# Experts 1 to 7: the first layer as seven block products in place of eight, in three passes over the tokens

## The chip, the cores and the metric

The kernel runs on one core of a Trainium2 chip, alone. The metric is the device time of one execution in microseconds (us), the median of three runs. Its engines are TensorE (PE, whose weight loads the profile shows apart as PEld), VectorE (DVE), ScalarE (ACT), GpSimd (POOL) and SyncE (SP, which issues all DMAs here). Each takes its instructions strictly in the order in which the program gives them; they wait for each other by semaphores.

## What is computed

Sparse attention feeds a mixture of experts with a Sinkhorn gate. Cut to what matters (x has 2304 rows, D = 512, 8 experts, F = 1024, all float32):

```python
x = attention(q, k, v)                  # 4 batches x 576 positions, 8 heads x 64
P = sinkhorn(exp(x @ w_gate), 8 rounds) # over all 2304 tokens
for e in range(8):
    h = np.maximum(x @ w1[e], 0.0)      # first layer, 512 -> 1024
    out += P[:, e:e + 1] * (h @ w2[e])  # second layer, 1024 -> 512
```

## The kernel before

Every operand of a large product is held as two float32r numbers, a high part (a copy that rounds) and a low part (the rest), and a product is three matmuls: high by high, high by low, low by high. The first layer of one f tile (128 columns of F) for a chunk of tokens is 4 blocks of D by 3 = 12 matmuls into one PSUM bank (`layer1`, L324 to L341); ACT writes relu's high part, DVE its low part. The second layer (`layer2`, L343 to L372) takes 3 matmuls for each 128 tokens and adds up four f tiles in a bank.

A unit is four f tiles, half an expert: 16 units. Unit 0 takes tokens in 9 chunks of 256; units 1 to 15 in four chunks of 512 and one of 256, which stands third (last in unit 15). A slot is one f tile of one chunk: `layer1` of this slot, then `layer2` of the slot before (L434 to L457). The attention of all batches (32 steps) is woven into the prologue and the first 26 slots of unit 0, the gate's 28 pieces into the 28 slots after those. Weights are loaded piece by piece through four raw buffers and split once each by ACT (L125) and POOL (L126) in the last chunk of the unit before. `xhi` and `xlo` hold all tokens in SBUF for the whole run (L95, L96); `acc` holds the output (L97).

The order on each engine is the order in which the code calls it (`manual_schedule`, L84); nothing moves it.

Of the kernel before, what the change touches and what calls it, by code (L numbers as in the profile page):

```python
# [14 lines left out]
S = 576  # L15
# [36 lines left out]
def kernel(  # L52
# [16 lines left out]
    FH = 4  # f tiles of a unit (half an expert)  # L69
# [30 lines left out]
    pieces = [(u, ft, which) for u in range(NU) for ft in range(FH) for which in range(2)]  # L100
# [3 lines left out]

    def load_w():
        nonlocal n_loaded
        if n_loaded == len(pieces):
            return
        u, ft, which = pieces[n_loaded]
        n_loaded += 1  # L110
        e, fh = divmod(u, UPE)
        f0 = (fh * FH + ft) * P
        t = raw_p.tile([P, D], F32, tag="raw", name=f"raw{which}_{u}_{ft}")
        if which == 0:
            t = t.rearrange("p (k f) -> p k f", f=P)
            nc.sync.dma_start(t, w1[e, :, f0 : f0 + P].rearrange("(k p) f -> p k f", p=P))
        else:
            nc.sync.dma_start(t, w2[e, f0 : f0 + P, :])
        raw[u, ft, which] = t

    def split_w(u, ft, which):
        src = raw.pop((u, ft, which))
        shape = [P, 2, NDT, P] if which == 0 else [P, 2, D]
        t = wt_p.tile(shape, F32R, tag=f"w{which + 1}", name=f"w{which + 1}_{u}_{ft}")
        nc.scalar.activation(t[:, 0], src, AF.Copy)  # L125
        nc.gpsimd.tensor_tensor(t[:, 1], src, t[:, 0].bitcast(F32), op=ALU.subtract)  # L126
        wt[u, ft, which] = t
        load_w()

# [1 line left out]
    # A tile holds, for a local pair, 64 queries of each head (partition halves) by the 96 keys of  # L131
    # their window; for a strided pair, one head's queries by keys of a group of residues.
# [5 lines left out]
    def load_qkv(k):  # L138
        if k < NS:
            nq, nk, nv = _columns(*steps[k][1:])  # L140
            t = qkv_p.tile([P, QK], F32, tag="qk", name=f"qk_{k}", bufs=3)
            nc.sync.dma_start(t[:, : nq + nk], qkv[k, :, : nq + nk])
            tv = qkv_p.tile([P, 5 * 2 * DH], F32, tag="v", name=f"v_{k}", bufs=5)
            nc.sync.dma_start(tv[:, :nv], qkv[k, :, nq + nk : nq + nk + nv])
            qkv_t[k] = t, tv[:, :nv].rearrange("p (w j d) -> p w j d", j=2, d=DH)

    def at_scores(k):
# [17 lines left out]
        else:  # L165
# [3 lines left out]
            # The heads use different row halves of the array and different banks. The first  # L169
            # batch takes one head after the other, so that its softmax starts sooner.  # L170
# [12 lines left out]
        for j, (sc, masks, n, rows, nk) in enumerate(res):  # L183
            sm = at_p.tile([P, 5 * KW], F32, tag="sm", name=f"sm_{k}_{j}", bufs=6)
# [14 lines left out]
            sms[k].append((sm, sums[:rows, j * n : (j + 1) * n], n, rows, nk))  # L199
# [11 lines left out]
    def at_transpose(k):  # L211
        pts[k] = []
        for j, (sm, _, n, rows, nk) in enumerate(sms.pop(k)):
            pt = at_p.tile([P, 5, P], F32, tag="pt", name=f"pt_{k}_{j}")
# [8 lines left out]
    def at_values(k, tag):  # L223
# [3 lines left out]
        if _is_local(p):  # L227
# [9 lines left out]
            src = pv[:, : n * QT]  # L237
            dst = [x[:, p, c0 : c0 + n * QT] for x in (xhi, xlo)]
        else:
            r0, nr, n = SGROUPS[hf]  # L240
            m = nr * NJ
            for i in range(n):
                for j in range(2):
# [6 lines left out]
            dst = [  # L250
                x[:, p, b * S : (b + 1) * S].rearrange("p (j r) -> p j r", r=STRIDE)[
                    :, :, r0 : r0 + nr * n
                ]
                for x in (xhi, xlo)
            ]
        nc.scalar.activation(dst[0], src, AF.Copy)  # L256
        nc.vector.tensor_tensor(dst[1], src, dst[0].bitcast(F32), op=ALU.subtract)  # L257

# [1 line left out]
    def gate_logits(c0, n):  # L260
        pl = ps.tile([P, 4 * P], F32, tag="t", name=f"pl_{c0}")
        for dt in range(NDT):
            for i, x in enumerate((xhi, xlo)):
                nc.tensor.matmul(  # L264
                    pl[:, :n], wgs[:, 2 * E * dt : 2 * E * dt + P], x[:, dt, c0 : c0 + n],
                    start=(dt == 0 and i == 0), stop=(dt == NDT - 1 and i == 1),
                )
        nc.vector.tensor_copy(lt[:, :n], pl[: 2 * E, :n])
# [55 lines left out]
    def layer1(u, c, ft):  # L324
# [11 lines left out]
        h = h_p.tile([P, 2, 4 * P], F32R, tag="h", name=f"h_{u}_{c0}_{ft}")  # L336
# [6 lines left out]
    def layer2(u, c, ft):  # L343
# [8 lines left out]
        for i in range(nt):  # L352
# [6 lines left out]
            if ft == FH - 1:  # L359
                t = c0 // P + i  # L360
                e = u // UPE
                if u == 0:
                    nc.scalar.activation(acc[:, t, :], y, AF.Copy)
                elif e == 0:
                    nc.vector.tensor_tensor(acc[:, t, :], y, acc[:, t, :], op=ALU.add)
                else:
                    nc.vector.scalar_tensor_tensor(  # L367
                        acc[:, t, :], y, gate[:, t, e : e + 1], acc[:, t, :],
                        op0=ALU.mult, op1=ALU.add,
                    )  # L370
                if u == NU - 1:
                    nc.sync.dma_start(out[t * P : (t + 1) * P, :], acc[:, t, :])  # L372

# [18 lines left out]
    def attention_values(tag="t"):  # L392
        if 0 <= at_k - LAG < NS:
# [13 lines left out]
    for k in range(2 * NP - 2 + LAG):  # L407
# [3 lines left out]
        if 1 <= k <= 2 * FH:  # L411
            split_w(*pieces[k - 1])
# [7 lines left out]

    slots = []
    for u in range(NU):
        if u == 0:
            chunks = [(c, 256) for c in range(0, NT, 256)]
        else:
            chunks = [(c, min(512, NT - c)) for c in range(0, NT, 512)]
            if u < NU - 1:
                chunks.insert(2, chunks.pop())
# [3 lines left out]
    bg = None  # L432
    prev = None
    for u, c, ft, last in slots + [(None, None, None, False)]:  # L434
        if u is not None:
            layer1(u, c, ft)
            if last and u + 1 < NU:
                split_w(u + 1, ft, 0)
# [4 lines left out]
        if u == UPE and ft == 2:  # L443
            for t in range(c[0] // P, (c[0] + c[1]) // P):
                nc.vector.tensor_scalar_mul(acc[:, t, :], acc[:, t, :], gate[:, t, 0:1])
        if prev is not None:
            pu, pc, pft, plast = prev
            layer2(pu, pc, pft)
            if plast and pu + 1 < NU:
# [7 lines left out]
        prev = (u, c, ft, last) if u is not None else None  # L457
# [79 lines left out]
```

## Time and profile before

| what | value |
|---|---|
| median of 3 runs | 1687.38 us (1685.89 to 1687.57) |
| the profiled execution, first to last instruction | 1686.0 us |
| TensorE busy | 1670.7 us, 99% |
| DVE, ACT, POOL busy | 494.6, 336.3, 200.2 us |
| mean granted TensorE clock | 0.996 of full speed |

A matmul row in a timeline has a start and a length; matmuls overlap, so the pace is read from one start to the next. The chain of waits is followed back from the last instruction: who ended last at each step. A window is a stretch of the span with each engine's busy time in it.

### The profile page before, as it was taken

The numbers are of one execution on the slowest core, as the hardware profiler recorded it, in microseconds if no ns is written. First come the engines' busy times: TensorE is split into PE (matmuls) and PEld (weight loads), VectorE is DVE, ScalarE is ACT, GpSimd is POOL, SyncE is SP. The second block draws the span as 40 slices with busy tenths as digits, with TensorE's granted clock in tenths as the row PEclk, the third lists the DMA queues.
The fourth block names the chain that finished last, engine by engine and source line by source line (L and its number), as shares of the span: only waits on it lengthen the run. The fifth ranks groups of instructions, "written<-read, shape, count | busy, mean of one in ns | idle before, by whom it ended". The sixth has DMA issues, their size and how long they took to land.

```text
span 1686.0 us, 20710 instructions
## 1 busy us (share of the span) xinstructions
PE 1670.7 (99%) x8611; PEld 1402.1 (83%) x8611; DVE 494.6 (29%) x1162; ACT 336.3 (20%) x824; POOL 200.2 (12%) x182
## 2 busy tenths in 40 slices
PE   7999999999999999999999999999999999999999
PEld 5888888888888888888888888888888888888887
DVE  4654244233222222222222222222222222222222
ACT  5554211112121111212111121211112121111211
POOL 4221200102020010202001020200102020010200
PEclk8999999999999999999999999999999999999999
DMA  6431100101010010101001010100101010010011
GB/s 208 127 104 50 45 7 13 38 1 51 0 45 7 13 39 0 51 0 44 7 14 38 1 50 1 44 7 13 37 1 51 1 44 7 13 38 1 26 50 63
DMA packets 55582, 56.80 MB, mean 34 GB/s; under 512 B 3904, under 2 KB 39744, under 8 KB 55488
## 3 DMA queue, kind: packets, MB, share of 16 engines
q1 hardware_dynamic: 55488, 55.47, 11.0%
q8 instruction: 68, 1.11, 0.3%
q14 instruction: 26, 0.21, 0.0%
HBM read 50.74 MB, written 4.72 MB: 33 GB/s over the span
## 4 chain that ended last, share of the span: by engine, by line
PE 98%; DMA 0%; POOL 0%; ACT 0%; DVE 0%; issue 0%; SPq 0%; POOLq 0%; ACTq 0%; DVEq 0%
PE ph L331 47%; PE y L355 47%; PE tp L219 1%; PE sc L159 1%; PE pv L232 1%; PE sc L176 1%; PE pl L264 0%; PE pv L244 0%; ACT sm L195 0%; DMA cst<-in_consts 0%; DMA qk<-in_qkv 0%; POOL w L126 0%; POOL sm L207 0%; PE pg L273 0%; DVE sm L189 0%
## 5 line engine op out<-in xcount | busy, mean ns | idle before, releaser
L355 PE MATMUL y<-w,h 128*128 128x512 f32 x3456 | 843.2, 391 | 0.0
L331 PE MATMUL ph<-xhi,w 128*128 128x512 f32 (+1 forms) x2688 | 787.8, 360 | 0.0
L355 PEld LDWEIGHTS y<-w,h 128*128 128x128 f32 x3456 | 642.5, 188 | 131.9
L331 PEld LDWEIGHTS ph<-xhi,w 128*128 128x128 f32 x2688 | 487.3, 189 | 77.4
L338 DVE SCALAR_TENSOR_TENSOR h<-ph,h 128x512 fp32r<-128x512 f32 (+1 forms) x336 | 206.8, 616 | 1110.1 <-ACT h L337 1110.1
L331 PE MATMUL ph<-xlo,w 128*128 128x512 f32 (+1 forms) x1344 | 482.6, 359 | 0.0
L337 ACT ACTIVATE h<-ph 128x512 fp32r<-128x512 f32 (+1 forms) x336 | 180.3, 537 | 1198.0 <-PE ph L331 1190.7
L126 POOL TENSOR_TENSOR w<-raw,w 128x512 fp32r<-128x512 f32 x128 | 164.7, 1287 | 1275.5 <-ACT w L125 1275.5
L331 PEld LDWEIGHTS ph<-xlo,w 128*128 128x128 f32 x1344 | 254.1, 189 | 39.6
L367 DVE SCALAR_TENSOR_TENSOR acc<-y,gate,acc 128x512 f32<-128x512 f32 x252 | 172.1, 743 | 1.2 <-PE y L355 1.2
L125 ACT ACTIVATE w<-raw 128x512 fp32r<-128x512 f32 x128 | 80.3, 627 | 101.2 <-POOL w L126 69.4
L195 ACT ACTIVATE sm<-sm,mx 128x96 f32<-128x96 f32 (+2 forms) x152 | 56.3, 372 | 33.5 <-DVE mx L189 33.5
L207 POOL TENSOR_TENSOR sm<-sm,sums 126x252 f32<-126x252 f32 (+3 forms) x48 | 35.2, 747 | 112.4 <-DVE sums L205 89.0
L189 DVE CUSTOM_DVE_ANT_0 sm<-sc,cst 128x96 f32<-128x96 f32 (+2 forms) x152 | 31.4, 264 | 12.2 <-DMA cst<-in_consts 5.9
L220 DVE COPY pt<-tp 126x252 f32<-126x252 f32 (+3 forms) x56 | 25.8, 494 | 20.0 <-PE tp L219 19.8
L195 ACT ACTIVATION_READ_ACCUMULATOR sm<-sm,mx 128x1 f32 (+2 forms) x152 | 28.4, 187 | 0.0
L219 PE MATMUL tp<-cst,sm 128*96 128x128 f32 (+2 forms) x152 | 23.8, 288 | 1.9 <-POOL sm L207 1.5
L219 PEld LDWEIGHTS tp<-cst,sm 128*96 128x96 f32 (+2 forms) x152 | 17.9, 139 | 7.7 <-POOL sm L207 3.5
L176 PE MATMUL sc<-qk 64*108 64x108 f32 (+1 forms) x160 | 15.9, 316 | 6.5 <-DMA qk<-in_qkv 4.2
L176 PEld LDWEIGHTS sc<-qk 64*108 64x108 f32 (+1 forms) x160 | 12.7, 208 | 8.6 <-DMA qk<-in_qkv 3.5
L257 DVE TENSOR_TENSOR xlo<-pv,xhi 128x252 fp32r<-128x252 f32 (+3 forms) x32 | 14.7, 458 | 15.0 <-ACT xhi L256 13.5
L159 PE MATMUL sc<-qk 64*64 64x96 f32 x288 | 17.6, 271 | 1.2 <-DMA qk<-in_qkv 1.2
(46 smaller groups left out, 185.2 us busy)
## 6 DMA issues: line engine op xcount, KB each, us to landing
raw<-in_w SPq DMA_DIRECT2D x128, 256.0 KB, 2.7
out<-acc SPq DMA_DIRECT2D x18, 256.0 KB, 2.0
qk<-in_qkv SPq DMA_DIRECT2D x8, 336.0 KB, 3.4
qk<-in_qkv SPq DMA_DIRECT2D x8, 324.0 KB, 3.1
v<-in_qkv SPq DMA_DIRECT2D x8, 320.0 KB, 2.9
qk<-in_qkv SPq DMA_DIRECT2D x8, 256.0 KB, 2.9
v<-in_qkv SPq DMA_DIRECT2D x8, 256.0 KB, 2.7
qk<-in_qkv SPq DMA_DIRECT2D x8, 252.0 KB, 3.1
```

The source lines that it names most:

```text
L125: nc.scalar.activation(t[:, 0], src, AF.Copy)
L126: nc.gpsimd.tensor_tensor(t[:, 1], src, t[:, 0].bitcast(F32), op=ALU.subtract)
L159: nc.tensor.matmul(sc[QT * j : QT * j + QT, i, :], t[sl, q0 : q0 + QT], t[sl, k0 : k0 + KW], start=True, stop=True,)
L176: nc.tensor.matmul(scs[j][:m, i, :m], t[sl, i * m : (i + 1) * m], t[sl, nq + i * m : nq + (i + 1) * m], start=True, stop=True,)
L195: nc.scalar.activation(sm[:, i, :], sm[:, i, :], AF.Exp, bias=mx[:rows, i : i + 1], scale=-1.0, accum_out=sums[:rows, j * n + i : j * n + ...
L207: nc.gpsimd.tensor_tensor(sm, sm, rs.unsqueeze(2).to_broadcast([rows, n, nk]), op=ALU.mult)
L219: nc.tensor.transpose(tp[:nk, i, :rows], sm[:, i0 + i, :], ident[:rows, :rows])
L331: nc.tensor.matmul(ph[:, :n], w[:, i, dt, :], x[:, dt, c0 : c0 + n], start=(k == 0), stop=(k == 3 * NDT - 1),)
L337: nc.scalar.activation(h[:, 0, :n], ph[:, :n], AF.Relu)
L338: nc.vector.scalar_tensor_tensor(h[:, 1, :n], ph[:, :n], 0.0, h[:, 0, :n].bitcast(F32), op0=ALU.max, op1=ALU.subtract)
L355: nc.tensor.matmul(y, h[:, a, i * P : (i + 1) * P], w[:, b, :], start=(ft == 0 and first), stop=(ft == FH - 1 and a == 1),)
L367: nc.vector.scalar_tensor_tensor(acc[:, t, :], y, gate[:, t, e : e + 1], acc[:, t, :], op0=ALU.mult, op1=ALU.add,)
```

## The change

Units 0 and 1 (expert 0) stay as they are. For experts 1 to 7 the first layer is cut in 2 by 2 blocks: x into token halves by halves of D, w1 into halves of D by halves of F. With s1 = x21 + x22, s2 = s1 - x11, s3 = x21 - x11, s4 = x12 - s2 and t1 = w12 - w11, t2 = w22 - t1, t3 = w12 - w22, t4 = w21 - t2, seven products and sums of their results give the four blocks of h that eight took.

- Tokens go in three passes of 768 (halves of 384, `TN`), and in each pass experts 1 to 7 go through in groups of two f tiles (one of each half of F): 3 x 7 x 4 = 84 groups. A group (`first`) has 7 products of 6 matmuls with 384 columns, and between them, as `fill(0)` to `fill(5)`, the second layer of the group before (`second`): 6 token tiles of 6 matmuls with 512 columns.
- DVE joins the products (`plus`, five times a group) and writes four low parts of relu; ACT copies one product and writes four high parts; DVE adds each of the 6 second-layer results to `acc` right away.
- w1 and w2 are loaded and split anew in each pass. POOL makes the t's of a group (three subtractions) and the low halves of w1's seven operands (four subtractions) and of two w2 tiles (two).
- x is written to DRAM (`store_x`, 2 MB for 512 tokens) as attention ends a chunk. While the gate runs, `build_s` makes the s's in six steps, one for each pass and each half of the 128-row blocks: four loads of x from DRAM, one POOL addition of 1536 columns (high plus low), four of 384, then an ACT copy of 1536 columns and a POOL subtraction of 1536, and two stores. One of its three parts runs at the end of each slot, from the 27th slot of unit 0 on. The region `reg` that held x then takes two sets of w1 operands and seven x operands, loaded for each pass by `load_x`.

```diff
+    def build_s(p, k):
+        st = pools["sb"].tile([P, 4, 2, TN], F32, tag="sx", name=f"sx_{p}_{k}", bufs=1)
+        t0 = 2 * TN * p
+        for i, (dh, th) in enumerate(((0, 0), (0, 1), (1, 1), (1, 0))):
+            nc.sync.dma_start(
+                st[:, i], xd[:, :, k + 2 * dh, t0 + TN * th : t0 + TN * (th + 1)]
+            )
+        yield
+        x, s = st[:, :, 0, :], st[:, :, 1, :]
+        nc.gpsimd.tensor_tensor(x, x, s, op=ALU.add)
...
+            nc.gpsimd.tensor_tensor(s[:, i, :], a, b, op=op)
+        yield
+        so = pools["sb"].tile([P, 2, 4, TN], F32R, tag="so", name=f"so_{p}_{k}", bufs=1)
+        split(so[:, 0], so[:, 1], s)
+        for i in range(2):
+            nc.sync.dma_start(sd[:, p, :, i, k, :], so[:, i].bitcast(F32))
+        yield
...
+    def prep_w1(g):
...
+        nc.gpsimd.tensor_tensor(
+            t, b[:, 0:1, :].to_broadcast([P, 2, 2 * P]), a, op=ALU.subtract
+        )
+        nc.gpsimd.tensor_tensor(u[:, 0], a[:, 1], t[:, 0], op=ALU.subtract)
+        nc.gpsimd.tensor_tensor(u[:, 1], b[:, 1], u[:, 0], op=ALU.subtract)
+        split(w[:, 0, 0:2], w[:, 1, 0:2], ra)
+        yield
+        split(w[:, 0, 4:6], w[:, 1, 4:6], ru)
+        yield
+        split(w[:, 0, 2:4], w[:, 1, 2:4], rt)
+        yield
+        split(w[:, 0, 6], w[:, 1, 6], rb[:, 1])
+        yield
...
+    def first(g, fill):
...
+        load_w1g(g + 2)
+        load_w2g(g + 1)
+        mul("w11", "x11", ba, True)
+        nc.scalar.activation(m1, A, AF.Copy)
+        mul("t2", "s2", bb, True)
+        plus(u2, B, m1)
+        mul("t1", "s1", bc, True)
+        fill(0)
+        w1n, w2n = prep_w1(g + 1), prep_w2(g)
+        mul("w21", "x12", ba, False)
+        relu_hi(0, 0, A)
+        relu_lo(0, 0, A)
+        next(w1n, None)
+        fill(1)
+        mul("t3", "s3", bb, False)
+        plus(u3, B, m1)
+        plus(u3, C, u3)
+        relu_hi(1, 1, u3)
+        next(w1n, None)
+        fill(2)
+        relu_lo(1, 1, u3)
+        fill(3)
+        mul("t4", "x22", bb, False)
+        plus(m1, B, m1)
+        relu_hi(1, 0, m1)
+        mul("w22", "s4", bc, False)
+        plus(u2, C, u2)
+        relu_hi(0, 1, u2)
+        relu_lo(1, 0, m1)
+        relu_lo(0, 1, u2)
+        next(w1n, None)
+        next(w2n, None)
+        fill(4)
+        next(w1n, None)
+        next(w2n, None)
+        fill(5)
...
             if at_k == NS + LAG:
-                bg = gating()
-        elif bg is not None:
-            next(bg, None)
+                store_x()
+                stacks["right"].close()
+                pools["sb"] = ctx.enter_context(tc.tile_pool(name="sb", bufs=1, side="right"))
+                bg = [gating(), sums()]
+        else:
+            for x in bg:
+                next(x, None)
+            if u == 1 and c[0] == 0 and ft == 0:
+                bg.append(early())
```

The change moves instructions at three places that matter below.

ACT, last chunks of unit 0, before (`h` is relu's high part of tokens from 1792 on, f tile by f tile; `acc` the copy of unit 0's result):

```order
L337 ACTIVATE h_0_1792_0_2395<-ph_0_1792_0_2382 128x256
L363 ACTIVATE acc_93<-y_0_1536_0_2314 128x512
L363 ACTIVATE acc_93<-y_0_1536_1_2315 128x512
L337 ACTIVATE h_0_1792_1_2429<-ph_0_1792_1_2416 128x256
L337 ACTIVATE h_0_1792_2_2459<-ph_0_1792_2_2446 128x256
L337 ACTIVATE h_0_1792_3_2491<-ph_0_1792_3_2478 128x256
L337 ACTIVATE h_0_2048_0_2519<-ph_0_2048_0_2506 128x256
```

and after (`so` is the split sum, first number the pass, second the half):

```order
L386 ACTIVATE h_0_1792_0_2469<-ph_0_1792_0_2456 128x256
L411 ACTIVATE acc_96<-y_0_1536_0_2371 128x512
L411 ACTIVATE acc_96<-y_0_1536_1_2372 128x512
L155 ACTIVATE so_0_0_2490<-sx_0_0_2418 128x1536
L386 ACTIVATE h_0_1792_1_2508<-ph_0_1792_1_2495 128x256
L386 ACTIVATE h_0_1792_2_2543<-ph_0_1792_2_2530 128x256
L386 ACTIVATE h_0_1792_3_2580<-ph_0_1792_3_2567 128x256
L155 ACTIVATE so_0_1_2595<-sx_0_1_2525 128x1536
L386 ACTIVATE h_0_2048_0_2613<-ph_0_2048_0_2600 128x256
```

The copies of the sums now stand between the relu's, one for three slots.

POOL at the same place, where before it had nothing between the last attention step (`sm`) and the splits of unit 1's weights; after:

```order
L245 TENSOR_TENSOR sm_31_0_2217<-sm_31_0_2217,sums_31_2216 128x480
L463 TENSOR_TENSOR sx_0_0_2418<-sx_0_0_2418 128x4x384
L471 TENSOR_TENSOR sx_0_0_2418<-sx_0_0_2418 128x384 x4
L156 TENSOR_TENSOR so_0_0_2490<-sx_0_0_2418,so_0_0_2490 128x1536
L463 TENSOR_TENSOR sx_0_1_2525<-sx_0_1_2525 128x4x384
L471 TENSOR_TENSOR sx_0_1_2525<-sx_0_1_2525 128x384 x4
L156 TENSOR_TENSOR so_0_1_2595<-sx_0_1_2525,so_0_1_2595 128x1536
L156 TENSOR_TENSOR w1_1_0_2616<-raw0_1_0_387,w1_1_0_2616 128x512
L156 TENSOR_TENSOR w1_1_1_2660<-raw0_1_1_495,w1_1_1_2660 128x512
L156 TENSOR_TENSOR w2_1_0_2673<-raw1_1_0_441,w2_1_0_2673 128x512
L463 TENSOR_TENSOR sx_1_0_2639<-sx_1_0_2639 128x4x384
```

The chain of additions and subtractions of a step stands ahead of the weight splits that follow it.

PE in the expert loop, after, one group (`ba`, `bb`, `bc` are the banks of the products, `yg` the second layer of the group before; before, 12 matmuls of `layer1` alternate with 12 of `layer2`):

```order
L555 MATMUL ba_20_6380<-reg_97 128x384 x6
L555 MATMUL bb_20_6381<-reg_97 128x384 x6
L555 MATMUL bc_20_6382<-reg_97 128x384 x6
L572 MATMUL yg_19_0_6413<-w2g_19_0_6349,h00_19_6230 128x512 x3
L572 MATMUL yg_19_0_6413<-w2g_19_1_6362,h01_19_6231 128x512 x3
L555 MATMUL ba_20_6380<-reg_97 128x384 x6
L572 MATMUL yg_19_1_6436<-w2g_19_0_6349,h00_19_6230 128x512 x3
L572 MATMUL yg_19_1_6436<-w2g_19_1_6362,h01_19_6231 128x512 x3
L555 MATMUL bb_20_6381<-reg_97 128x384 x6
```

The second layer of a group follows three products after the end of that group's own products.

## Rows read from the trace of the kernel before

**Rows 1.** The page's first part (busy us, share of the span, instructions) and the engine line of its chain that ended last.

```profile
PE 1670.7 (99%) x8611; PEld 1402.1 (83%) x8611; DVE 494.6 (29%) x1162; ACT 336.3 (20%) x824; POOL 200.2 (12%) x182
...
PE 98%; DMA 0%; POOL 0%; ACT 0%; DVE 0%; issue 0%; SPq 0%; POOLq 0%; ACTq 0%; DVEq 0%
```

**Rows 2.** Chain of waits in order of time: the 12 second-layer matmuls behind the chunk of 256 in units 2 and 3 (start, length, what).

```profile
347.85 2.75 PE y L355 x12
446.17 2.75 PE y L355 x12
```

**Rows 3.** Timeline of PE and its weight loads in unit 2 (start us, length, engine, line, form, count): 12 matmuls of 512 columns of layer 1, 12 of layer 2, 12 of 256 columns of layer 1, 12 of layer 2; each PE row is the first of its kind, and one weight load stands between.

```profile
340.81 0.39 PE L331 MATMUL ph<-xhi,w 128*128 128x512 f32 x1
...
343.53 2.88 PE L355 MATMUL y<-w,h 128*128 128x512 f32 x12
...
346.25 0.28 PE L331 MATMUL ph<-xhi,w 128*128 128x256 f32 x1
346.26 0.19 PEld L331 LDWEIGHTS ph<-xlo,w 128*128 128x128 f32 x1
...
347.69 2.91 PE L355 MATMUL y<-w,h 128*128 128x512 f32 x12
```

**Rows 4.** Groups of instructions with shapes kept apart (line, engine, operation, tile, shapes, count, busy us, mean ns of one, idle before).

```profile
L367 DVE SCALAR_TENSOR_TENSOR acc<-y,gate,acc 128x512 f32<-128x512 f32 x252 | 172.1, 743 | 1.2 <-PE y L355 1.2
...
L126 POOL TENSOR_TENSOR w<-raw,w 128x512 fp32r<-128x512 f32 x128 | 164.7, 1287 | 1275.5 <-ACT w L125 1275.5
...
L337 ACT ACTIVATE h<-ph 128x512 fp32r<-128x512 f32 x240 | 143.5, 598 | 956.2 <-PE ph L331 952.7 <-DVE g L298 3.5
...
L125 ACT ACTIVATE w<-raw 128x512 fp32r<-128x512 f32 x128 | 80.3, 627 | 101.2 <-POOL w L126 69.4 <-PE y L355 31.8
...
L337 ACT ACTIVATE h<-ph 128x256 fp32r<-128x256 f32 x96 | 36.8, 383 | 241.8 <-PE ph L331 238.0 <-DVE g L295 3.8
...
L207 POOL TENSOR_TENSOR sm<-sm,sums 126x252 f32<-126x252 f32 x16 | 9.4, 606 | 34.0 <-DVE sums L205 17.2 <-ACT sm L195 8.7 <-ACT acc L363 8.1
...
L207 POOL TENSOR_TENSOR sm<-sm,sums 128x480 f32<-128x480 f32 x8 | 7.9, 988 | 27.3 <-DVE sums L205 25.7 <-DVE wgs L416 1.6
```

**Rows 5.** The same view for DVE alone: two shapes of a subtraction with one input in PSUM.

```profile
L257 DVE TENSOR_TENSOR xlo<-pv,xhi 128x320 fp32r<-128x320 f32 x8 | 3.9, 490 | 2.8 <-ACT xhi L256 2.8
...
L257 DVE TENSOR_TENSOR xlo<-pv,xhi 128x256 fp32r<-128x256 f32 x8 | 3.4, 425 | 3.9 <-ACT xhi L256 3.0
```

**Rows 6.** Timeline around 300 to 306 us in unit 2's first slots: relu's high part on ACT, the split of a weight on ACT and POOL, and from 305.23 the last of 12 matmuls and the relu that waits for it.

```profile
300.21 0.60 ACT L337 ACTIVATE h<-ph 128x512 fp32r<-128x512 f32 x1 [2.04 <-PE ph L331]
300.71 0.62 ACT L125 ACTIVATE w<-raw 128x512 fp32r<-128x512 f32 x1
...
301.41 1.28 POOL L126 TENSOR_TENSOR w<-raw,w 128x512 fp32r<-128x512 f32 x1 [1.86 <-ACT w L125]
...
305.23 0.39 PE L331 MATMUL ph<-xhi,w 128*128 128x512 f32 x1
...
305.65 0.60 ACT L337 ACTIVATE h<-ph 128x512 fp32r<-128x512 f32 x1 [2.04 <-PE ph L331]
```

**Rows 7.** Timeline of DVE's scaling of `acc` (L445, four instructions in each row) without POOL at work and with it, and of POOL at the second place.

```profile
372.57 1.67 DVE L445 TENSOR_SCALAR acc<-acc,gate 128x512 f32<-128x512 f32 x4
...
394.29 1.29 POOL L126 TENSOR_TENSOR w<-raw,w 128x512 fp32r<-128x512 f32 x1 [1.86 <-ACT w L125]
394.33 3.81 DVE L445 TENSOR_SCALAR acc<-acc,gate 128x512 f32<-128x512 f32 x4
...
396.57 1.29 POOL L126 TENSOR_TENSOR w<-raw,w 128x512 fp32r<-128x512 f32 x1 [1.00 <-ACT w L125]
```

**Rows 8.** DMA: the GB/s of 40 equal slices of the first 10 us, all queues of the span (packets, MB, share of 16 engines), and two kinds of issue with the us from issue to landing.

```profile
GB/s 0 0 0 0 0 0 0 129 113 258 376 386 250 152 180 131 169 304 208 231 340 342 361 348 337 348 366 348 328 346 348 358 361 369 358 363 361 361 381 369
...
q1 hardware_dynamic: 55488, 55.47, 11.0%
...
raw<-in_w SPq DMA_DIRECT2D x128, 256.0 KB, 2.7
out<-acc SPq DMA_DIRECT2D x18, 256.0 KB, 2.0
```

**Rows 9.** Timeline at the end of the attention (its last low part), the first matmul of the 29th and 30th slots of unit 0, and in unit 1 the first matmul of the tenth slot and, behind it, the 6 `layer2` matmuls of the ninth.

```profile
163.62 0.49 DVE L257 TENSOR_TENSOR xlo<-pv,xhi 128x320 fp32r<-128x320 f32 x1 [0.37 <-ACT xhi L256]
...
172.45 0.39 PE L331 MATMUL ph<-xhi,w 128*128 128x256 f32 x1
...
177.21 0.28 PE L331 MATMUL ph<-xhi,w 128*128 128x256 f32 x1
...
250.89 0.28 PE L331 MATMUL ph<-xhi,w 128*128 128x256 f32 x1
...
252.32 1.56 PE L355 MATMUL y<-w,h 128*128 128x512 f32 x6
```

**Rows 10.** Stretches in the prologue with each engine's busy time; PEclk, the granted clock as a share of full speed, is the third number from the right.

```profile
22.00:24.00 2.00, 1.25 (x12) 0.73 (x8) 0.75 (x9) 1.69 (x9) 1.81 (x3) 1.00 0.92 250
24.00:26.00 2.00, 0.83 (x10) 0.68 (x10) 1.48 (x5) 0.64 (x2) 1.00 (x2) 0.65 0.71 232
26.00:28.00 2.00, 2.00 (x26) 1.78 (x24) 0.66 (x7) 0.28 (x1) 1.89 (x2) 0.50 0.86 314
```

More of the change, by code (lines that the diff above doesn't have):

```diff
@@ L236, in at_values @@
             c0 = b * S + ws[0] * QT
-            src = pv[:, : n * QT]
-            dst = [x[:, p, c0 : c0 + n * QT] for x in (xhi, xlo)]
+            moves = [
+                (pv[:, t - c0 : t - c0 + m], [xv(i, p, t, m) for i in range(2)])
+                for t, m in pieces(c0, n * QT)
+            ]
         else:
@@ L371, in layer2 @@
-                if u == NU - 1:
-                    nc.sync.dma_start(out[t * P : (t + 1) * P, :], acc[:, t, :])
+    TN = 3 * P
+    NPASS = NT // (2 * TN)
+    FP = F // (2 * P)
+    W1N = 7 * 2 * 2 * P
+    XN = 2 * 2 * TN
+    XOPS = ("x11", "s2", "s1", "x12", "s3", "x22", "s4")
+    at = W1N
+    w1_at, x_at = [0], {}
+    for name in XOPS[:3]:
+        x_at[name] = at
+        at += XN
+    x_at["x12"] = 4 * 2 * NDT * CH
+    for name in XOPS[4:]:
+        x_at[name] = at
+        at += XN
@@ new lines @@
+    w1_at.append(at)
+    assert at + W1N <= x_at["x12"] and x_at["x12"] + XN <= 2 * NDT * NT
+    wops = [
+        reg[:, o : o + W1N].rearrange("p (i m k f) -> p i m k f", i=2, m=7, k=2) for o in w1_at
+    ]
+    W_AT = {"w11": 0, "w22": 1, "t1": 2, "t3": 3, "t2": 4, "t4": 5, "w21": 6}
+    xops = {
+        name: reg[:, o : o + XN].rearrange("p (i k t) -> p i k t", i=2, k=2)
+        for name, o in x_at.items()
+    }
+    SOPS = ("s1", "s3", "s2", "s4")
+    sd = dram.tile([P, NPASS, len(SOPS), 2, 2, TN], F32, name="sd")
@@ new lines, in prep_w2, with product @@
+    def prep_w2(g):
+        if g >= NG:
+            return
+        w2s[g] = []
+        for i, src in enumerate(w2raw.pop(g)):
+            t = w2_p.tile([P, 2, D], F32R, tag="w2", name=f"w2g_{g}_{i}")
+            split(t[:, 0], t[:, 1], src)
+            w2s[g].append(t)
+            yield
+    def product(w, x, out, start):
+        n = 0
+        for k in range(2):
+            for i, xi in ((0, 0), (0, 1), (1, 0)):
+                nc.tensor.matmul(
+                    out[:, :TN], w[:, i, k, :], xops[x][:, xi, k, :],
+                    start=(start and n == 0), stop=(n == 5), skip_group_check=True,
+                )
+                n += 1
@@ new lines, in second @@
+    def second(g, i):
+        if g < 0:
+            return
+        p, e, j = groups[g]
+        y = ps.tile([P, D], F32, tag="ys"[i % 2], name=f"yg_{g}_{i}")
+        hv = hg[g][i // 3]
+        o = (i % 3) * P
+        n = 0
+        for f in range(2):
+            for a, b in ((0, 0), (0, 1), (1, 0)):
+                nc.tensor.matmul(
+                    y, hv[f][:, a, o : o + P], w2s[g][f][:, b, :], start=(n == 0), stop=(n == 5)
+                )
+                n += 1
+        t = 6 * p + i
+        nc.vector.scalar_tensor_tensor(
+            acc[:, t, :], y, gate[:, t, e : e + 1], acc[:, t, :], op0=ALU.mult, op1=ALU.add
+        )
+        if e == E - 1 and j == FP - 1:
+            nc.sync.dma_start(out[t * P : (t + 1) * P, :], acc[:, t, :])
+        if i == 5:
+            del hg[g], w2s[g]
@@ new lines, in first, with mul, plus, relu_hi @@
+    def first(g, fill):
+        p, e, j = groups[g]
+        last = e == E - 1 and j == FP - 1
+        w = wops[g % 2]
+        h = [
+            [pools["hg"].tile([P, 2, TN], F32R, tag="hg", name=f"h{i}{f}_{g}") for f in range(2)]
+            for i in range(2)
+        ]
+        hg[g] = h
+        m1, u2, u3 = (
+            pools["u"].tile([P, TN], F32, tag=x, name=f"{x}_{g}") for x in ("m1", "u2", "u3")
+        )
+        ba, bb = (ps.tile([P, 4 * P], F32, tag="l1", name=f"b{x}_{g}") for x in "ab")
+        bc = ps.tile([P, 4 * P], F32, tag="t", name=f"bc_{g}")
+        A, B, C = (x[:, :TN] for x in (ba, bb, bc))
+        def mul(wn, xn, bank, start):
+            product(w[:, :, W_AT[wn]], xn, bank, start)
+            if last:
+                load_x(p + 1, xn)
+        def plus(o, bank, s):
+            nc.vector.tensor_tensor(o, bank, s, op=ALU.add)
+        def relu_hi(i, f, src):
+            nc.scalar.activation(h[i][f][:, 0], src, AF.Relu)
+        def relu_lo(i, f, src):
+            nc.vector.scalar_tensor_tensor(
+                h[i][f][:, 1], src, 0.0, h[i][f][:, 0].bitcast(F32), op0=ALU.max, op1=ALU.subtract
+            )
+        load_w1g(g + 2)
[34 more added lines that the diff above has]
+        fill(5)
+        next(w1n, None)
+        next(w2n, None)
@@ L419, with sums, early @@
         )
+    def sums():
+        for p in range(NPASS):
+            for k in range(2):
+                yield from build_s(p, k)
+    def early():
+        load_w1g(0)
+        for _ in range(9):
+            yield
+        yield from prep_w1(0)
+        load_w2g(0)
+        for name in XOPS[:3]:
+            load_x(0, name)
     slots = []
-    for u in range(NU):
+    for u in range(UPE):
         if u == 0:
@@ L431 @@
                 slots.append((u, c, ft, ci == len(chunks) - 1))
-    bg = None
+    bg = []
     prev = None
[L434 to L438, printed above, removed]
+    for u, c, ft, last in slots:
+        layer1(u, c, ft)
+        if last and u + 1 < UPE:
+            split_w(u + 1, ft, 0)
         busy = at_k < NS + LAG
@@ L448 @@
             layer2(pu, pc, pft)
-            if plast and pu + 1 < NU:
+            if plast and pu + 1 < UPE:
                 split_w(pu + 1, pft, 1)
```

195 lines of the change are left out of this document (150 added, 45 removed).

## The prediction

> **What bounds the kernel now.** The page's totals come first: TensorE is busy 99% of the span, and the chain that ended last is 98% PE [rows 1]. The order of time says whether that is one state or an average: the same place of units 2 and 3 lies 98.32 us apart [rows 2], so 14 units of experts 1 to 7 take 1376 of the 1686 us, at an even pace. What sets the pace? Twelve 512-column matmuls of the first layer take 343.53 - 340.81 = 2.72 us, or 226.7 ns each, twelve of the second layer the same, and twelve of 256 columns 347.69 - 346.25 = 1.44 us, or 120 ns [rows 3]. Columns cost 106.7 ns per 256, and 13.3 ns come on top of each matmul. The weight load between lasts 190 ns, yet matmuls start every 120 ns: loads overlap, and don't bound. A 384-column matmul then lies on the line between: 173.3 ns. So time goes with columns, and fewer columns are worth their share as long as nothing else ends last.
>
> **What the change takes from TensorE.** Per unit the first layer has 192 matmuls of 512 columns and 48 of 256: 192 x 0.2267 + 48 x 0.120 = 49.28 us, over 14 units 689.9 us. After, 84 groups have 42 matmuls of 384: 84 x 7.28 = 611.5 us. That removes **78.4 us**. The second layer keeps its 3024 matmuls. A group's own time without stalls is 7.28 + 36 x 0.2267 = 15.44 us.
>
> **What the sums of x cost.** In-order ACT gets, once in three slots, a copy that waits for POOL, with the relu of all later slots behind it; the second layer needs those, and TensorE stops one slot later. So the six steps of build_s are a serial chain. One step:
> - DMA: the low-half store (0.79 MB) and the next four loads (1.57 MB) go out together. A saturated core moves about 350 GB/s [rows 8], so 6.7 us, and of the 2.0 to 2.7 us to landing of 0.26 MB some 1.3 to 2.0 are fixed: 8.7 us.
> - POOL's additions: 512 columns take 1287 ns; the line through 252 (606) and 480 (988) has 184 ns fixed [rows 4]. With that fixed part 1536 columns take 3.49 us and 384 take 1.01; 3.49 + 4 x 1.01 and hand-overs: 7.7 us. I take the 1287 row as nearest, since it has two full operands. Ends: along the cheaper row 2.76 and 0.83, in proportion to the 1287 row 3.86 and 0.97.
> - ACT's copy: 627 ns for 512 [rows 4], and 0.84 ns a column from 598 and 383: 1.5 us, with hand-over 1.6.
> - POOL's low half: 3.5 us, with hand-over 3.6.
>
> Together 21.6 us. The first step starts when attention ends at 164.1 [rows 9]; the last stores of x (3.15 MB) are ahead of its loads on the same rings: 2.0 + 4.72 MB / 350 = 15.5 us, then 7.7 and 1.5: its copy ends at 188.8, while it stands behind the relu of the slot that began at 172.45. Five more steps: 296.8. In between come two POOL splits of unit 1's weights and 0.8 MB of weight loads on SP's queue ahead of loads of x: 4 us. The last copy ends near 300.8 and the relu behind it at 301.4; its second-layer matmuls stood at 252.32 [rows 9]. TensorE loses **49 us**, and 2 us more because it restarts slowly: after sparse work the granted clock was 0.50, the 1.2 GHz level, at 26 us [rows 10]; in the earlier steps this is hidden, as three slots (16.3 us) and 2 us fit into 21.6. Ends of this term: with the cheap POOL row and 389 GB/s a step is 18.0 us and the loss 26; with the dear row and the 299 GB/s of the whole span (55.47 MB at 11.0% of 1686 us) a step is 23.6 and the loss 64.
>
> The Trainium skill, GPSIMD Engine Reference, section 3.1, gives 4497 ns for an addition of 2048 float32 columns; scaled, an estimate of 3.4 us for 1536. By it the step would be about 1 us shorter and the loss about 45. No run here shows that size.
>
> **The hand-over between two groups.** The second layer of group g starts after three products of group g+1 and needs the low half of the second w2 tile at its fifth matmul. Count from the end of the last product. Its sum on DVE starts 0.2 us later (305.65 against the last start at 305.23 plus 0.21 [rows 6]) and takes 0.56, from 490 and 425 ns [rows 5]; relu on ACT 0.52; the copy of the t's 0.6, overlapping 0.1 as at 300.71; POOL starts 0.08 after ACT [rows 6]; then three low halves of 512 and one of 256 columns, 3 x 1.29 + 0.74 = 4.6. That makes 6.5 us. TensorE has two fills of 1.36, three products of 1.04 and four matmuls until then: 6.75. A margin of 0.1 to 0.25 us is less than I can price; POOL to PE has no row here. I take 0.05 us a group, **4 us**, with ends 0 and 0.3 us a group (25). Nothing is gained here: TensorE can't run ahead of its columns. Elsewhere in a group the engines have room: POOL 7.5 x 1.29 = 9.7 us, DVE 9 x 0.56 + 6 x 0.74 = 9.5, ACT 5 x 0.5 + 5.5 x 0.63 = 6.0, of 15.44; a group's 1.05 MB of weights need 3 us.
>
> **The rest.** Group 0 has no second layer to lie between its products. There DVE has four additions and six scalings ahead of the sums that free the banks, then the splits follow late: worked out in the same prices, the first group's second layer ends 5 to 7 us late; I take **6** (3 to 9). At two pass switches DVE scales 6 tiles of acc while POOL is at work. Four scalings took 1.67 us alone and 3.81 against two POOL splits [rows 7]: 2.1 us for two. Six against some six POOL instructions are held until 6 to 7 us into the next group, and the third product needs a sum behind them: 2.5 us each, **5** (0 to 10). Seven x operands (5.5 MB) per switch need 16 us at 350 GB/s and have 23 until the last is used; nothing. Stores of x during attention (2.1 MB, 6 us) lie ahead of loads that are needed 10 us later; nothing, or 2 us each. At the end the last second layer follows its products at once: **1**.
>
> **Sum.** 1686.0 - 78.4 + 49 + 2 + 4 + 6 + 5 + 1 = 1674.6 us. The profiled time stands 1.4 us below the median of 1687.38, so I forecast **1676 us**, 0.7% faster.
>
> **The rivals.**
> 1. *The sum chain is short.* If POOL's wide additions go along the cheaper row and the DMAs overlap better, the loss is 26 instead of 51: 1651 us. For it: 389 GB/s in single slices. Against it: the 1287 row has operands like these. Chance 0.14.
> 2. *The chain stalls nothing* (the change is as good as its columns): 1687.4 - 78.4 + 16 = 1625 us. It needs a step below the 9 to 16 us of three slots; the two 1536-column passes and four 384s alone are 11 us on POOL. Chance 0.04.
> 3. *The hand-over is late, and the kernel slower than before.* Place: the fifth matmul of fill(0), on POOL's last low half. Price: each 0.1 us is 8.3 us in 83 groups; it decides from (1690.8 - 1676) / 83 = 0.18 us on. A DVE and a POOL instruction can hold each other up, as [rows 7] show for L445; if one 0.56 us relu low part is held in front of, or holds, POOL's chain, the margin of 0.1 becomes -0.45: 38 us, 1714. For it: three low parts a group read two SBUF operands, a form that no POOL instruction meets in this trace; in my count one ends at 14.6 us of the group and POOL starts at 14.6. Against it: those low parts start first. Chance 0.20. The Trainium skill (SBUF — State Buffer, section "Who interferes with whom") says that a DVE instruction with two SBUF inputs contends with a GpSimd instruction that reads SBUF, the earlier one blocking the other; by that rule these three are exposed. L445's wait at 394.33 agrees with the lock.
> 4. *The chain is longer* (64 us and more): 1690 us, about where it was. Chance 0.08.
>
> **How the numbers follow.** My forecast holds 0.54; within its own terms it spans 1662 to 1692. Below 0.2% (1684.0, about what a measurement of this kernel can tell from no change) lie 0.43 of it and rivals 1 and 2: 0.61. Within 0.2% (to 1690.8): 0.08 of it and half of rival 4: 0.12. Above: 0.03 of it, rival 3 and the other half of rival 4: 0.27. The range: to leave out no more than 0.2, from 1649 (rival 1) to 1706 (rival 4 and the cheaper half of rival 3).
>
> **What would show it.** In the changed profile: 384-column matmuls starting every 173 ns, and 42 of them in 7.3 us; six PE gaps of some 8 us between 180 and 305 us, each ended by ACT behind a 1536-column copy, 21 to 22 us apart; group periods of 15.4 to 15.6 us; the clock at 0.5 after each gap. The prediction is wrong if the copies come much closer together than 20 us, if the groups take over 15.7 us, or if a 384-column matmul starts every 190 ns, paced by its weight load.

## The result and the profile after

The changed kernel takes **1700.74 us** (median of 4 runs, 1699.3 to 1701.88) against 1687.47 of the kernel before: a ratio of 1.0081, 95% interval 1.0067 to 1.0096. It is 0.8% slower, where 0.7% faster was forecast. The profiled execution spans 1699.8 us.

The page's totals, and the engines of the chain that ended last:

```profile
PE 1633.4 (96%) x8779; PEld 1446.0 (85%) x8779; DVE 942.0 (55%) x1914; ACT 586.9 (35%) x1386; POOL 958.4 (56%) x862
...
PE 86%; POOL 4%; DMA 3%; DVE 2%; issue 2%; SPq 1%; ACT 1%; POOLq 0%; ACTq 0%; DVEq 0%
```

TensorE is busy for only 37 us less than in [rows 1], though its columns are worth 78, and the chain that ended last (the work followed back from the last instruction) is no longer PE's alone. Where POOL and DMA come in, the chain in order of time shows (start us, length, engine or queue and what):

```profile
170.66 8.31 DMA sx<-xd
179.22 3.47 POOL sx L463
182.76 2.90 POOL sx L471 x3
185.72 1.00 POOL sx L471
186.75 1.49 ACT so L155
188.31 3.46 POOL so L156
...
195.00 6.27 DMA sx<-xd
201.43 3.49 POOL sx L463
...
300.94 0.99 POOL sx L471
...
304.17 2.39 DVE acc L413 x4
...
309.47 2.76 PE ph L380 x12
```

These are the sums of x. The additions of the first step end at 186.72, those of the sixth at 301.93: 23.0 us a step. Loads, additions, copy and low half follow each other and never overlap. The last row is TensorE's restart: twelve 256-column matmuls in 2.76 us, against 1.44 in [rows 3]. The stretch up to there has a granted clock of 0.81, in its last microseconds 0.50, and the one behind it 1.00 (PE's busy time is the first number behind the length, PEclk the third from the right):

```profile
180.00:313.00 133.00, 92.21 (x397) 74.66 (x396) 32.61 (x69) 23.60 (x38) 76.81 (x47) 0.81 0.43 142
309.00:311.00 2.00, 2.00 (x10) 2.00 (x11) 0.83 (x4) 0.00 (x0) 0.74 (x2) 0.50 0.54 194
313.00:360.00 47.00, 47.00 (x213) 38.53 (x212) 19.16 (x48) 6.68 (x13) 4.61 (x4) 1.00 0.38 130
```

The expert loop's first product starts at 360.99 (first line), where unit 2 of the kernel before starts at 302.73 (second line, from the trace of before):

```profile
360.99 1.23 PE L555 MATMUL ba<-reg 128*128 128x384 f32 x6
```

```profile
302.73 0.39 PE L331 MATMUL ph<-xhi,w 128*128 128x512 f32 x1
```

Then one group of the loop, in the same chain, from its first product to that of the next group:

```profile
396.64 1.06 PE ba L555 x6
397.71 1.04 PE bb L555 x6
398.75 1.04 PE bc L555 x6
399.79 1.39 PE yg L572 x6
401.18 1.06 PE ba L555 x6
402.24 1.39 PE yg L572 x6
403.63 1.06 PE bb L555 x6
404.69 2.79 PE yg L572 x12
407.48 1.05 PE bb L555 x6
408.54 1.04 PE bc L555 x6
409.58 2.77 PE yg L572 x12
412.35 1.06 PE ba L555 x6
```

It lasts 15.71 us, and so do all groups but the first two and the two in which DVE scales. It is PE from end to end: nothing waits. Yet 15.44 was expected, and the rows tell which part is slow. Twelve 512-column matmuls take 2.77 to 2.79 us, or 231 to 232.5 ns each, where [rows 3] have 226.7; seven products of 384 columns take 7.35 in place of 7.28. What TensorE does wait for in the whole run (waiter, releaser, us, times, longest):

```profile
PE y L404 <- ACT h L386: 25.5, 4, 7.8
PE y L404 <- ACT acc L411: 7.8, 1, 7.8
...
PE y L404 <- DVE acc L413: 6.5, 1, 6.5
...
PE yg L572 <- POOL w2g L156: 1.2, 2, 1.0
```

The last of them is the hand-over, which costs nothing in a steady group. The first three belong to the sums: six gaps, as many as were forecast, of 6.6 us on average in place of some 8. And 15.71 lies just over the 15.7 us that the prediction named as a sign of being wrong.

### The profile page after: what moved, and what is told of

It reads as the page before. It is cut to its first block, busy times and chain, and to the rows that moved or that the text cites. A ratio compares the mean times of both kernels' runs of the same rounds, so it can differ in the third digit from the quotient of the medians.

```text
span 1699.8 us, 23976 instructions
## 1 busy us (share of the span) xinstructions
PE 1633.4 (96%) x8779; PEld 1446.0 (85%) x8779; DVE 942.0 (55%) x1914; ACT 586.9 (35%) x1386; POOL 958.4 (56%) x862
## 4 chain that ended last, share of the span: by engine, by line
PE 86%; POOL 4%; DMA 3%; DVE 2%; issue 2%; SPq 1%; ACT 1%; POOLq 0%; ACTq 0%; DVEq 0%
PE yg L572 40%; PE bb L555 15%; PE ba L555 10%; PE bc L555 10%; PE y L404 4%; PE ph L380 4%; DMA sx<-xd 2%; POOL sx L471 1%; POOL sx L463 1%; SPq L458 1%; POOL so L156 1%; DVE acc L772 1%; PE tp L257 1%; PE sc L197 1%; PE pv L270 1%
## 5 line engine op out<-in xcount | busy, mean ns | idle before, releaser
L572 PE MATMUL yg<-w2g,h 128*128 128x512 f32 x3024 | 755.8, 394 | 1.4 <-POOL w2g L156 1.2
L572 PEld LDWEIGHTS yg<-w2g,h 128*128 128x128 f32 x3024 | 564.2, 188 | 105.8 <-POOL w2g L156 3.6
L577 DVE SCALAR_TENSOR_TENSOR acc<-yg,gate,acc 128x512 f32<-128x512 f32 x504 | 377.8, 750 | 246.5 <-PE yg L572 246.5
L555 PE MATMUL bb<-reg 128*128 128x384 f32 x1512 | 307.3, 338 | 6.1 <-DVE u L608 6.1
L555 PEld LDWEIGHTS bb<-reg 128*128 128x128 f32 x1512 | 272.0, 188 | 21.8 <-DVE u L608 7.3
L156 POOL TENSOR_TENSOR reg<-ru,reg 128x512 fp32r<-128x512 f32 x84 | 120.8, 1438 | 204.1 <-ACT reg L155 199.2
L156 POOL TENSOR_TENSOR w2g<-r,w2g 128x512 fp32r<-128x512 f32 x168 | 217.5, 1295 | 11.2 <-ACT w2g L155 11.2
L555 PE MATMUL ba<-reg 128*128 128x384 f32 x1008 | 205.8, 339 | 0.6 <-ACT m L621 0.6
L555 PE MATMUL bc<-reg 128*128 128x384 f32 x1008 | 203.1, 335 | 0.6 <-POOL reg L156 0.6
L404 PE MATMUL y<-w,h 128*128 128x512 f32 x432 | 122.3, 428 | 39.7 <-ACT h L386 25.5
L404 PEld LDWEIGHTS y<-w,h 128*128 128x128 f32 x432 | 84.7, 204 | 61.7 <-ACT h L386 33.6
L156 POOL TENSOR_TENSOR reg<-ra,reg 128x512 fp32r<-128x512 f32 x84 | 108.9, 1296 | 35.6 <-ACT reg L155 35.5
```

Source lines behind the costliest of these rows:

```text
L156: nc.gpsimd.tensor_tensor(lo, src, hi.bitcast(F32), op=ALU.subtract)
L404: nc.tensor.matmul(y, h[:, a, i * P : (i + 1) * P], w[:, b, :], start=(ft == 0 and first), stop=(ft == FH - 1 and a == 1),)
L555: nc.tensor.matmul(out[:, :TN], w[:, i, k, :], xops[x][:, xi, k, :], start=(start and n == 0), stop=(n == 5), skip_group_check=True,)
L572: nc.tensor.matmul(y, hv[f][:, a, o : o + P], w2s[g][f][:, b, :], start=(n == 0), stop=(n == 5))
L577: nc.vector.scalar_tensor_tensor(acc[:, t, :], y, gate[:, t, e : e + 1], acc[:, t, :], op0=ALU.mult, op1=ALU.add)
```

## The experiments

Times are medians; the kernel before took 1686.87, 1686.54 and 1686.13 us beside the three sets of runs. Modulo 256 bytes, the addresses of the tiles that the experts' matmuls read differ in one respect: in the kernel before all of them begin at a multiple of 256 bytes in their partition; in the changed kernel the small tiles of the `st` pool (896 bytes) now lie ahead of w1 and h, which so begin 128 bytes off, while x, w2 and the seven w1 operands don't.

**e1: addresses.**

```diff
+    st_p.tile([P, 32], F32, tag="pad", name="pad", bufs=1)
     pools = {}
```

> The changed kernel with 128 unused bytes per partition ahead of the tiles that hold w1, h and all that follows them, so that every tile that TensorE loads as weights begins at a multiple of 256 bytes, as in the kernel before (in the changed kernel h begins 128 bytes off). Address theory: 512-column matmuls settle to 226.7 ns after some six matmuls, as in the kernel before, a group falls from 15.71 to 15.55 to 15.65 us, the time by 5 to 13 us to 1688 to 1696. Rival, alternation of widths (384 and 512 in short runs) keeps TensorE out of its even pace: no change, 1701. Rival, DVE and POOL work beside it slows TensorE: no change, 1701.

Measured: 1694.34, ratio to the kernel before 1.0043 (1.0031 to 1.0056), 6.4 us less than the changed kernel. The chain of a group:

```profile
396.76 1.39 PE yg L573 x6
...
401.62 2.76 PE yg L573 x12
```

Twelve take 2.76 and the first six 1.39, so the last six take 1.37: settled. Without the 128 bytes it was 2.79 - 1.39 = 1.40 (1.38 in the group's other such row): never settled. The group falls to 15.64, near the upper end of what was expected, and 0.20 stay. So addresses matter, but are the smaller part; the rest is what e4 and e10 are about.

**e2: the same, put into the kernel before.**

```diff
     acc = big.tile([P, NTT, D], F32, name="acc")
+    big.tile([P, 32], F32, name="pad")
```

> The kernel before with 128 unused bytes per partition ahead of the weights and h; nothing else differs. Address theory: 512-column matmuls no longer settle and take 232 ns as in the changed kernel, 408 of them a unit at 5.5 ns more, 2.2 us a unit, 15 units: 1687 + 33 = 1720. Rivals (alternation of widths, work of DVE and POOL): no change, 1687.

Measured: 1709.32, ratio 1.0132 (1.0116 to 1.0147). 128 unused bytes cost 22.5 us. The chain in unit 1:

```profile
332.26 2.79 PE ph L332 x12
335.05 2.73 PE y L356 x12
```

Only the first layer stays slow. There the weights (w1) are shifted and the moving tile (x) is not; in the second layer weights (h) and moving tile (w2) are shifted alike. It is the distance between the two that counts, not the address of one, and that is why the price is two thirds of the 33 us expected: by the starts in the trace some 17 us are the first layer's 2880 matmuls at 6 ns more, and most of the rest the first three matmuls of each second-layer run (232, 233 and 231 ns; then 227).

**e4: the widths, in the kernel before.**

```diff
-            chunks = [(c, min(512, NT - c)) for c in range(0, NT, 512)]
-            if u < NU - 1:
-                chunks.insert(2, chunks.pop())
+            chunks = [(c, 384) for c in range(0, NT, 384)]
```

> The kernel before with units 1 to 15 in six chunks of 384 columns in place of four of 512 and one of 256: the widths 384 and 512 alternate as in the changed kernel, with none of its POOL and DVE work and aligned weights. A unit's matmuls at the even pace are 24 x (12 x 173.3 + 9 x 226.7) = 98.9 us. Address theory: runs of 512 settle at 226.7 ns from the seventh matmul on, unit 99.5 to 100.2 us, 1705 to 1716. Alternation theory: 512-column matmuls stay at 231 to 232 ns through all nine, unit 100.4 us or more, 1718. Theory of DVE and POOL work: 226.7 ns from the first on, unit 98.9, 1696.

Measured, in one run: 1718.21; a unit takes 100.48 us, where the even pace gives 98.9. The chain:

```profile
404.25 2.10 PE ph L331 x12
406.35 2.08 PE y L355 x9
```

Nine of 512 columns take 231 ns each, twelve of 384 take 175, with good addresses and without the changed kernel's work on POOL and DVE. The starts in the trace show a transient, an uneven stretch before the pace settles: behind a change to 512 columns they lie 229, 233, 236, 224, 231, 236, 228, 233 and 231 ns apart, 41 ns in all above nine at 226.7; behind a change to 384 they lie 171, 175, 178, 185, 176 and 181 ns apart and then 173, 26 ns above. My number for settling (the seventh) was too early; in e1's runs of twelve it is the tenth (227 ns), so the nine here never get there.

**e10: one width, in the changed kernel.**

```diff
-                    y, hv[f][:, a, o : o + P], w2s[g][f][:, b, :], start=(n == 0), stop=(n == 5)
+                    y[:, :384], hv[f][:, a, o : o + P], w2s[g][f][:, b, :384],
+                    start=(n == 0), stop=(n == 5),
```

> The aligned version with second-layer matmuls of 384 columns in place of 512 in experts 1 to 7: 128 of the 512 output columns are left out there, so that all matmuls of the loop have one width, beside the same work on ACT and POOL and nearly the same on DVE. Theory of the alternation: 78 matmuls a group at 173.3 ns, 13.52 us, plus waits that the profile shows on POOL's low half (the hand-over has 5.9 us of TensorE's time now for its 6.4 us): each 384-column matmul that waits for nothing starts 173 or 174 ns after the one before. Rival (work of DVE, POOL and DMA beside it slows TensorE): 175 to 177 ns on average as in the changed kernel, also far from waits.

Measured, in one run: 1573.12. Between waits the matmuls start 173 or 174 ns apart, 173.7 on average with the few behind a wait. The chain and the wait on POOL:

```profile
741.03 2.08 PE yg L573 x12
```

```profile
PE yg L573 <- POOL w2g L157: 35.4, 85, 1.1
```

With one width the transient is gone, beside the same work of POOL and ACT. A group takes 14.21 in place of 13.52, since the hand-over is now late in every one. So its chain is about as long as worked out (6.5 us), and in the changed kernel it is the longer fills, of 512 columns, that hide it.

**e7: another distance.** The pad of e1 with 48 in place of 32 words.

> The aligned version with 192 unused bytes in place of 128: w1 and h begin 64 bytes off a multiple of 256. If the pace needs a multiple of 256 (or of 128 with the moving tile), 512-column matmuls don't settle, 1699 to 1702 as in the changed kernel; if only a distance of 128 is bad, they settle as in the aligned version, 1694.

Measured, in one run: 1705.37, 3 us past the range expected, and a group takes 15.76. The chain:

```profile
734.82 2.80 PE yg L573 x12
```

64 bytes off is worse than 128 (15.71); of the three distances tried only a multiple of 256 settles.

**e3: no sums.**

```diff
         for p in range(NPASS):
-            for k in range(2):
-                yield from build_s(p, k)
+            yield
...
-        if name in SOPS:
-            nc.sync.dma_start(o, sd[:, p, SOPS.index(name)])
...
+        if True:
+            th, dh = (int(name[1]) - 1, int(name[2]) - 1) if name not in SOPS else (0, 1)
```

> The changed kernel without build_s: nothing makes the s's, and blocks of x itself are loaded in their place, so the output is not the reference's; all else runs. Theory of the sums' chain: the expert loop begins at 303 to 306 us as the unit does in the kernel before, in place of 361.0, so 1701 - 55 to 58 = 1643 to 1646. Rival: something else is late next (weights and x of the first group, loaded and split in the same slots), and the loop begins at 312 or later: 1652 and more.

Measured: 1645.33, ratio 0.9754 (0.9741 to 0.9767). The loop begins at 304.82, so the sums cost 56.2 of the 58.3 us; the other 2.1 are the slower 512-column matmuls of units 0 and 1 (it begins at 302.53 where e6 below aligns them). Nothing else is late there.

**e8: ACT's copy moved to POOL.**

```diff
-        split(so[:, 0], so[:, 1], s)
+        nc.gpsimd.tensor_copy(so[:, 0], s)
+        nc.gpsimd.tensor_tensor(so[:, 1], s, so[:, 0].bitcast(F32), op=ALU.subtract)
```

> The changed kernel with the 1536-column copy of each sum step on POOL in place of ACT; steps, places and loads stay. Theory (the chain costs because in-order ACT holds relu behind the copy): the slots run ahead while POOL works, the chain still ends near 305, the loop begins at 308 to 318 us in place of 361, 1648 to 1658. Rival (the sums themselves end last, whoever copies): the loop begins no earlier than 350, 1690 to 1710.

Measured: 1694.65, ratio 1.0047 (1.003 to 1.0063); the loop begins at 356.37. The theory in this form fell: the copy is gone from ACT, and ACT still stands. What it and PE wait for:

```profile
ACT w L155 <- DMA raw<-in_w: 33.6, 3, 21.4
ACT reg L155 <- POOL ru L532: 32.7, 1, 32.7
```

```profile
PE y L404 <- DVE acc L413: 26.7, 1, 26.7
PE ph L380 <- POOL w L156: 14.1, 2, 12.2
```

Unit 1's weights are loaded on SP's queue behind loads of x that wait for their buffer, and split on POOL behind the additions; the first group's t's and u's stand on POOL behind the whole chain, with ACT's copy of `ru` waiting for them and relu behind that. The chain holds three in-order queues, and the copy was only the first place where it showed. The rival held: the loop begins behind 350 us and the time lies within 1690 to 1710, and the chain that ended last runs through the sums' loads and POOL's instructions up to 312 us. What it leaves open is how the sums can get out of the way; e9 and e5 show two ways.

**e9: two load buffers.** `sx` gets `bufs=2`, and each step's loads are issued two steps ahead.

> The changed kernel with two buffers for the loads of the sums: a step's loads are issued two steps ahead, right behind the copy that frees the buffer, so that they lie beside POOL's work; all six steps stay ahead of the expert loop, a part at the end of every slot from the same slot on. Theory (a step is serial, 8 to 9 us of loads, then 7.5 of additions, 1.5 of copy, 3.5 of low half, and everything on ACT, POOL and SP queues behind it): a step falls from 23 to 13 to 15 us, about the three slots of 16 us that it stands in, and most of the stall goes: loop at 312 to 325 us in place of 361, 1652 to 1665. Rival (POOL's work or the store of the sums sets the step): a step stays over 18 us, loop at 335 or later, 1675 and more.

Measured: 1668.92, ratio 0.9896 (0.9879 to 0.9912); the loop begins at 328.03, 3 us past the range expected, and the time is 4 us past its own. The steps' wide additions start at 180.32, 192.82, 209.20, 226.51, 239.18 and 254.79: 14.9 us a step in place of 23.0. With loads beside the additions the chain loses 33 us, and already beats the kernel before.

**e5: sums out of the way.** Two of six steps ahead of the loop, with gaps; the other four in quarters at the end of groups 1 to 16.

```diff
+            for n, _ in zip(slots_of, build_s(0, k)):
+                for _ in range(n):
+                    yield
...
+        if g:
+            next(late, None)
```

> The changed kernel with the sums spread out: only pass 0's two steps are made before the expert loop, their parts 1 to 4 slots apart in place of one after every slot; the four steps of passes 1 and 2 are made in the loop, one quarter of a step at the end of each of groups 1 to 16. Theory of the chain (it costs because ACT's copy stands in front of relu and waits for DMA and POOL): the loop begins at 305 to 312 us in place of 361, POOL takes the late parts in its idle 6 us a group, 1645 to 1652. Rival: the late parts stand on POOL in front of the weights' low halves and hold the hand-over by 1 to 3 us in 16 groups, 1660 to 1700.

Measured: 1645.62, ratio 0.9757 (0.9742 to 0.9772). It takes as long as without sums: the loop begins at 304.65, and the groups with a late part take 15.71 like all others.

**e6: all of it.** e5, the pad of e1, and `scale(0)` behind group 0.

> The one before with two more edits: the 128 unused bytes of the aligned version, and the scaling of acc's first six tiles moved on DVE from ahead of group 0's sums to behind them. Alignment is worth 6.4 us (measured alone), the scaling at most its 2.97 us on the chain of group 0: 9 us below the spread version, 1636 to 1643. Rival: the scaling is hidden by POOL's splits, which then end last: 6 us below it.

Measured: **1633.83**, ratio 0.9689 (0.9674 to 0.9703), the fastest, 11.8 us below e5 where 9 were expected, and 2 us below the range. The loop begins at 302.53, 2.1 us earlier than in e5, and a group takes 15.64. Of the first groups the chain shows:

```profile
309.79 2.39 DVE acc L414 x4
312.18 0.46 DVE h L616
...
321.11 1.41 POOL w2g L157
...
322.57 0.73 PE yg L574 x2
```

DVE goes on to h at once, where the changed kernel has six scalings in between:

```profile
364.30 2.79 PE y L404 x12
367.11 0.50 ACT m L621
...
368.26 2.39 DVE acc L413 x4
370.65 2.97 DVE acc L772 x6
...
383.49 1.23 POOL w2g L156
384.77 0.72 PE yg L572 x2
```

From the loop's start to the first second-layer matmul behind POOL's last low half it is 384.77 - 360.99 = 23.8 us there and 322.57 - 302.53 = 20.0 here. Both end on POOL's splits, but these start earlier; the rival is out. The gain of 3.8 us is more than the 2.97 allowed for.

The second chain shows a wait that stays in e6 and that I had not named: ACT's first copy (`m`) begins at 367.11, right behind the last of unit 1's second-layer matmuls, while its product ended at 362.21. DVE's sum, additions and scalings follow in order. No run tested why the copy waits; its pool takes the place of those that held unit 1's w1 and h.

## Why the prediction was wrong

The sum said 1674.6, the profiled execution took 1699.8. Term by term, in us:

| term | forecast | measured |
|---|---|---|
| columns, at the even pace | -78.4 | -78.4 (by count) |
| sums of x, restart included | +51 | +58.3 (56.2 without the 2.1 of pace in units 0 and 1) |
| pace in 84 groups, (15.707 - 15.44) x 84 | not in the sum | +22.4 |
| hand-over | +4 | 0 |
| groups 0 and 1: 17.37 - 10.0 (products and twelve matmuls of 512 at the even pace) and 18.12 - 15.71 | +6 | +9.8 |
| two pass switches, 1.10 each | +5 | +2.2 |
| end | +1 | about 0 |

The right column gives 1686.0 + 14.3 = 1700.3. The 1700.74 us lie inside the stated range, which reached 1706 only for rivals 3 and 4; neither is what happened, so that is luck.

**The step that failed** is "a group's own time without stalls is 7.28 + 36 x 0.2267 = 15.44 us", with "the second layer keeps its 3024 matmuls" ahead of it. I took a pace from long runs of one width, and put it under runs of 6 to 18 matmuls that alternate between two; the measured group is 15.71 us. e4 and e10 show that the alternation itself costs: 0.20 us a group (15.64 - 15.44 in e1), 16.8 us in all. Another 0.07 us a group, 5.6 us, come from where the tiles lie, which neither the diff nor the profile names (e1, e2). The first could have been read before: the second-layer row of [rows 2], behind a chunk of 256, is 2.75 us long, while the same twelve take 2.72 in [rows 3] behind a chunk of 512. I used that row for a period only. The line of widths I drew from [rows 3] was right for a settled run: 173.3 ns was measured.

**The chain of sums** was right as a mechanism and 7 us short. Its first copy ends at 188.24 (188.8 forecast), additions take 7.5 us (7.7), the copy 1.49 (1.6), the low half 3.46 (3.6); loads are landed 9.5 us after the low half's end (8.7), and splits of weights stand between, so that a step takes 23.0 (21.6). That puts the last copy 2.6 us late. 2.1 us are the pace of units 0 and 1, and the other 2.5 the restart, by DVE's four waiting additions and the half clock. The dear POOL row (1287 ns) was the right one to take: 1536 columns took 3485 ns where the line with 184 ns fixed gave 3.49 us. The Trainium skill's figure (GPSIMD Engine Reference, section 3.1), scaled to an estimate of 3.4 us, agrees with this within 4%. That ACT is where the chain reaches TensorE held for this kernel, but not as the one place (e8).

**Rival 1** (a short chain) and **rival 2** (no stall) didn't occur here; e9 and e5 built them. **Rival 3**, the slower one, gave the right sign by the wrong mechanism: POOL's last low half ends before the fifth matmul of `fill(0)`. The timeline of a later group (start, length):

```profile
728.65 1.30 POOL L156 TENSOR_TENSOR w2g<-r,w2g 128x512 fp32r<-128x512 f32 x1
...
729.47 1.55 PE L572 MATMUL yg<-w2g,h 128*128 128x512 f32 x6
```

POOL ends at 729.95, the fifth matmul starts at 729.47 + 4 x 0.231 = 730.39: a margin of 0.44 us, where 0.1 to 0.25 was worked out; about 0.1 us of it is there because TensorE is slower. Of the three low parts of relu one meets POOL: in this group it runs from 720.92 to 721.47 and POOL's split of the u's from 721.17, the other two have ended by the time POOL's next split starts at 725.46. That split of the u's takes 1438 ns on average, the other two of that form 1296 and 1298. The Trainium skill's rule of the shared port (SBUF — State Buffer, section "Who interferes with whom") agrees in kind; here it costs 0.14 us, on a split that nobody waits for. **Rival 4** (a longer chain, 64 us and more) didn't occur: the 58.3 us lie about halfway between it and the forecast.

**Groups 0 and 1** were 4 us dearer than forecast: the six scalings, which I counted, lie on the chain with their full 2.97 us, the splits behind them follow with gaps for ACT's copies, and the late first copy (367.11) was not in my working. An estimate from the rows: without it DVE's four additions could end 0.6 us behind the last second-layer matmul (367.09), where they end at 370.65, some 3 us later. No run moved that copy. **The pass switches** were cheaper: each is 1.10 us, so DVE's six scalings are mostly covered.

## What to carry to other kernels

A matmul's price read from long runs of one width isn't its price in short runs of alternating widths; look in the profile before for the row behind a change of width. When tiles move in memory, compare the pace of work that didn't change (here the second layer of unit 1): a shift of 128 bytes cost 22 us in a kernel otherwise untouched. Background work shares in-order queues with the main loop; where its result is needed late, spread it out in short pieces: four of the six sums had hundreds of microseconds of time, and spread out they cost nothing (e5 takes 1645.62 us, without sums it is 1645.33).

## What was not expected of the hardware

Behind a change of width TensorE's starts lie unevenly: behind nine or twelve of 512 columns for six matmuls of 384 (26 ns in all), behind 384 columns for nine of 512 (41 ns; e4, e1). It depends on what went before: behind six of 512 it is 4 ns in e1, and behind 256 columns, in the kernel before, 28 ns over five of 512. With weights and moving tile 128 or 64 bytes apart (modulo 256), 512-column matmuls did not settle in runs of up to twelve: 231 to 233 ns in place of 226.7. What in the chip does this the runs don't show, nor whether other distances are good; only 0, 64 and 128 were tried.
